# Moving elementwise steps between VectorE and GpSimd in a scheduled four-layer attention kernel

## The chip, the core and the metric

The kernel runs on one core of one Trainium2 chip. The metric is the device time of one execution in microseconds (us). The core's engines run their own instruction streams and wait for each other by semaphores: TensorE (PE) for matmuls, ScalarE (ACT) for activations, VectorE (DVE) and GpSimd (POOL) for elementwise work, and SyncE (SP), which here only issues DMAs.

## The reference

x is one sequence of 2048 tokens with 512 features, in bfloat16. Two kinds of layer alternate, each added to its input after a layer normalization, and each kind is applied twice with the same weights. Heads: 32 of 16 features.

```python
x = x + A(layernorm(x)); x = x + B(layernorm(x))     # twice

def A(x):     # four segments of 512 tokens, M and z carried from one to the next
    for s in range(4):
        p = softmax(q_s @ k_s.T * scale + causal_mask);  a_dot = p @ v_s
        a_mem = (phi(q_s) @ M) / (phi(q_s) @ z + 1e-6)   # phi(t) = t + 1 if t > 0 else exp(t)
        o = g * a_mem + (1 - g) * a_dot                  # g = sigmoid(beta), by head
        M = M + phi(k_s).T @ v_s;  z = z + phi(k_s).sum()
    return o @ wo

def B(x):     # linear attention, not causal
    phi = lambda t: concat(softmax(t @ w_phi), softmax(-t @ w_phi))
    kv = phi(k).T @ v;  z = phi(k).sum()
    return ((phi(q) @ kv) / (phi(q) @ z + 1e-6)) @ wo
```

## The kernel before

The sequence is held in SBUF as X, 16 tiles of 128 tokens. The program first records every operation as a node of a graph: the tiles that it reads and writes, the engines on which it may run, and for each engine a duration and a function that issues it. `Graph.place` then takes a packed table (`ORDER`) that holds, for all operations, their order, the engine of each, and the buffer of each tile; `Graph.emit` writes out one stream per engine with the semaphore waits that follow. So the order of everything, the choice between engines and the buffers come from that table, and an operation can only stand on an engine for which it has an entry.

The steps that the change and the prediction speak of:

- `ln` normalizes one tile of 128 tokens: statistics on VectorE (L599, L600), then on GpSimd an addition of epsilon (L607) and the power -1/2 (L609), then `xn = (x - mean) * rstd` on VectorE (L620, tile p). A transpose follows, by DMA from SP (L364) or, for some tiles, on TensorE (L380) with an evacuation (L359 on ScalarE, L360 on VectorE, tile pX).
- `a_proj` projects K, Q and V of a segment (L341). `kmask` then multiplies K with four masks of heads (L686 on VectorE, or L688 on ScalarE for a few) into pQ, the weights of the score matmuls. `phi` computes phi(t) as min(max(t, 0) + 1, exp(t)): the exponential on ScalarE, the clamp (max and add, L674) and the minimum (L675) on VectorE.
- `a_att`: scores (L326), their exponentials on ScalarE (L351, tiles p and pP), the product with V (L326), the division (L393, L906) and, from the second segment on, the addition of the memory part (L910). `out_proj` multiplies with wo and adds to X (L961).
- `b_keys` and `b_query` do layer B: exponentials on ScalarE (L351), sums and divisions on VectorE (L1015, L1030, L1117), V into pT (L359 or L360), and the sum of the two halves of the numerator (L1123).

`D` is the PSUM buffer, of which there are four. GpSimd otherwise makes constants and clears buffers, most of it at the start. The functions that the change touches, and what calls them:

Of the kernel before, what the change touches and what calls it, by code (L numbers as in the profile page):

```python
# [10 lines left out]
ALU = mybir.AluOpType  # L11
# [5 lines left out]
D = 512  # L17
H = 32
# [279 lines left out]
class Kernel:  # L298
# [58 lines left out]

    def evac(self, out_ap, in_ap, n, reads, writes, opens=(), label="", fast=False):
        ch = {"act": (n / 1.2 + 51, lambda e: e.activation(out_ap(), in_ap(), ACT.Copy)),  # L359
              "dve": ((340 if fast else n / 0.96 + 65), lambda e: e.tensor_copy(out_ap(), in_ap()))}  # L360
        return self.g.op(ch, reads, writes, opens, label=label, port=fast)
# [232 lines left out]
    def ln(self, t, xT, flex=False, pe=False, root="pool"):  # L594
# [24 lines left out]
        else:  # L619
          v(lambda e: e.tensor_scalar(xn.t[:], self.X[:, t, :], self.mv[:, t, 0:1], self.rstd[:, t:t + 1],  # L620
                                    op0=ALU.subtract, op1=ALU.mult), 300,
# [45 lines left out]
    def phi(self, dst, src, e_, keys, c0, n):  # L667
# [6 lines left out]
        v(lambda e: e.tensor_scalar(cut(dst), cut(src), 0.0, 1.0, op0=ALU.max, op1=ALU.add), 68 + n / 3.84, S, D, label="phmax", port=True)  # L674
        v(lambda e: e.tensor_tensor(cut(dst), cut(dst), cut(e_), ALU.min), 68 + n / 1.92, D + E, D, label="phadd", port=True)  # L675

    def kmask(self, KM, KT, halves, act):
# [3 lines left out]
        for sl in range(4):  # L681
# [4 lines left out]
            ch = {"dve": (129 + n / 3.84, lambda e, sl=sl, out=out: e.tensor_scalar(out(), src(), self.m4[:, sl:sl + 1], None, op0=ALU.mult))}  # L686
            if act:
                ch["act"] = (93 + n / 1.2, lambda e, sl=sl, out=out: e.activation(out(), src(), ACT.Copy, scale=self.m4[:, sl:sl + 1]))  # L688
# [150 lines left out]
    def a_att(self, L, s, i0):  # L839
# [10 lines left out]
        for gg in range(2):  # L850
# [58 lines left out]
            if s >= 1:  # L909
                v(lambda e, part=part: e.tensor_tensor(part(o), part(o), part(tmp), ALU.add), 335, [o[gg], tmp], [o[gg]], label="oadd", port=True)  # L910
# [139 lines left out]
    def b_query(self, L, c, store):  # L1050
# [49 lines left out]
        for tt in range(4):  # L1100
# [21 lines left out]
            if not pair:  # L1122
              v(lambda e, Tm=Tm, o=o: e.tensor_tensor(o.t[:].rearrange("p (a c) -> p a c", a=4), half(Tm, 0), half(Tm, 1), ALU.add), 335, [Tm], [o], label="nadd", port=True)  # L1123
# [56 lines left out]

def basep(ap):
# [13 lines left out]
TOK = {0: ((0, 1, 2, 3),), 1: ((0, 1, 2, 3),), 2: ((0, 1, 2, 3),), 3: ((0, 1, 2), (3,))}  # L1195
PE_T = ({("xA", 0, t) for t in range(4)} | {("xB", L, 15) for L in range(2)} | {("a", L, 3, 2, 1) for L in range(2)}
# [10 lines left out]
c-q~01C%YvvUWtIvs$OSk8RtwZQHhO+qP}nwr$&fRlCpJnYnk?y!+O_-oMs;xqDYuRz^lfeDOu>tkrRVL1IV_0QI0g5Hx^>&<LVIV`u_Rp&2xXWDp(VLOiGjnV~wAhxkweBxHk<Py<Rq  # L1207
R%ih&p%o~o3AvyGRD^<12y#MeXal987PN&jPzl;W3@8f;pfD7H_Rs-pLs38|1~H*Bl!M~X5n@3d=mec1AtZwAkOQhfUFZ!dAr)BY0=Xdxe1{+K6RN^%2!uD_Krr-yx6l_1e1z067}CHX
0PG3_;3**Xhj-8qy1@__3Q6G^aOe&LAvfm1_wWfm!xtC@d9erdgo%(3d%-l!iNhcl22lp^1H$z%12@2Q3`c`dz)YMA&*23O#t9GvmOemn%m}&IJa`GOU?Y^kuP_|Oz$WO2{V|wAXex|`
qF4+^!Z%m~4n=}3Fb#&_e8|E!!*&<}L(z}6LP?wsJ760`qX9SvRzWHBCx**lCuD)yFbQYEK->iyRs+XbFc||eEzE!^7=%k9I*o<Xum;NGR1|1&5|qUPxEzXLK`e|FFdXK`wJ;3JVLm8>  # L1210
XQ4E%gF?6hD&k5Qj`MH?#-K_V4#vTJ91j675+}oc9EDThFzkl|cmy1bKnLI;B*f7eKt~}MBhnr?2{CCe&cWTV4`*Q_j75>i4`<^7*b9j<KkS1EI0iGpSk$O+F)YO;I2RjW6I_gouo^bR
g_sVSVpLd()$u$mz{6-TB}OKRXJ8fXqKP;T7r}Tez?R{1Jc3nlH>JWxSQ%?z3P_Dru`$NRwOA9Qz(qJf>o5vkfJ+buS5bXT$7*41tcwew9yZ5=6c^LOYKo76R0mt&IoOOXu^G0)E!Y}Q
;wjvSo6sMUV0es&$MFQV!M1n^{4oTh(sc->qZoh@@CNLm^SA@EvIH0rFW@oUircXr?xo|f4WnZkTtk=P3be<A7!5-)Hm#-b)B$(nYCMN~Fa{ojLwFX~;Ck$cJ@5>6!VTD(R$wGNjXg0L
uArTmo@HQdXcxxBmb8*mP-pCd4e26Y!pIm4yJCGxj@>XNMa5Rsi1twpN<}HK0bRzV7>D*#FYJwduqL&o+EkZnQ9FuDQLqjbWc6qX#iQJ;J6?q=cnvyJV!A;$X(@G~tGJ0aQv$k%*YPek
rzX^xhEgXQM$M=%wx=6-6K`P%+<|-8fjUwP8crjqDRrf5^cd4(H@c74X(Yv`6EKRN-~-HxPcb9Dz=!w@vtcGIK$-C+X2;&thk8;kDoCeb5GAB#G=Y{=dc2K~Fas8%@$?+W&^Q`MqbVJB
r~cHJ22ej*M`I}om7pWEo`%q1I!YVp4i=`8l!x7djg*Z|q)C*Wm7-&GoDNYA)`Jey7D`H~X&X(Zt@Ie4KoR<ciRc}D#*8d4drx0*I~8Kz@fGI4T=W+2P(GHM^3V@FOH=48zM<E+gU--h
+DRv<Fnde)=p@~z+famEp=30bp3!M4%F@s&x=P>h9G$02G>x9qbh=Ep=n%`qa<bc$kKW@0I?O&%F?vK<@Dlq>KauDuy}`@uF{Put^om~72TV^#*hf6d($YivK}G2+eW3jGg)&eFmYIE|
($tY9r@`zA{iGpmAmfyuU1NjT3lcPsGSWM|&fM}vFX;xGPYdWKW7L&(W8dfkNy-b~Nzp~hN(WeR%0$4BX<A6xs4O#dkPT%g*f3U(on&RHCmYE|u@P(r^<v#wZ$@l58^g-89;_l8&B{|5
%1*b~ZN}IDR)J2jiqwboW96tX%L6&75@n%dtUo)=j<cCGi)Pb4wx1PaIcO}q!ZK5FHjZ6ol6PWfSP7>1ImX#Nc8AR&!S1tCtTL5klD%R6>>+!=?y^Pnmd$04*hMyvy<&4IfZc>D^q9S7
^Vw5Yl`gOa>^xh@7O`rix#5Z}rdo{iv+N10PMQgB*hDsoJ!8*VZ5GIa*i;t6CbMbmAyi;>SSXvqR<Q8QvZd@1L}JU>bQXbiW=q&CHk*}Ui`h&TjzxsX%wfyf3^s>#VJlf>R+o)ud)O+r  # L1220
m#t>?nB`TN!yB+qEPzL04Ovwd$S1Hh>;r4WKC>3=Bm2TyvTrPue`TdvHP(uKXZ4vMkIs;X=l(pHy<m;mJNBLhaW}NQ5(~%uSVXp#wPv&UIyQp?59YIZQ#O;oWb0X39)U;XA-o)K&Z@H?
Y#Uq0f3osC5|7L`u=PA9tI4*rjVubU&MWXKyaun$>+l_HCyT{mux4x%+svl&(mW2U$z!uNEG{d?%kaBUi^pS4SaDv7Z(;R$72c3n<Ox|--iWtjyI6cykJsf<St3@MH{kc68lS@(^Qb%m
v}e)yCO(%p;U)NPwwagYt9Ue4im&F;c?_PIZQ)z_R<?jI<kR?co|MPu^LP!GfUn`ncw4rE&*!`NTAqqe;*<GOo}8!VJ9z@ulsDrEc?!OWU*p&LV!n)b=81S>-i0sWyLl3pf-UDO_)4CP
# [76 lines left out]
```

## Time and profile before

| what | value |
|---|---|
| runs | 456.9, 456.93 and 458.73 us; median 456.93 |
| span of the profiled execution | 454.8 us; no time of its own is listed beside it |
| clock granted to TensorE | 1.000 over the span |
| GpSimd: busy, instructions | 58.4 us, 146 |
| VectorE: busy, instructions | 403.1 us, 766 |

A page of the profile gives busy time, share of the span and number of instructions by engine. A row of a group has the source line, engine, operation, what is written from what, the shapes and the count; then the busy time of the group in us and the mean of one in ns; then the idle time of the engine just before these instructions and what ended it. A row of a timeline begins with start and length in us. A row of waits says who waited, for whom, the total in us, how often, and the longest. The end of a matmul is modelled, and a GpSimd span is rough.

### The profile page before, as it was taken

The page shows a single profiled execution, that of the slowest core. Times are in us where ns is not written, and L with a number is a line of the kernel's source. Part 1 is how long each engine was busy: PE and PEld are TensorE (multiplying, and loading weights), DVE is VectorE, ACT ScalarE, POOL GpSimd, SP SyncE. Part 2 cuts the span into 40 slices and gives each one's busy share as a digit, 9 for nine tenths or more (in the row PEclk, how much of TensorE's full clock was granted, in tenths as well). Part 3 has the DMA queues.
Part 4 walks back from the last instruction along what each step waited for, and adds up shares of the span by engine and source line. Part 5 has one row for each costly group of instructions (what it writes and reads, how often), then busy time and mean ns, then how long its engine had stood idle before and what let it go on. Part 6 is the DMA issues. An engine that isn't in the chain of part 4 may idle for free.

```text
span 454.8 us, 26184 instructions
## 1 busy us (share of the span) xinstructions
PE 427.2 (94%) x12085; PEld 289.5 (64%) x12085; DVE 403.1 (89%) x766; ACT 420.9 (93%) x584; POOL 58.4 (13%) x146
## 2 busy tenths in 40 slices
PE   8999999999999989989999998999999988999787
PEld 4756667767766666655556666677677666765444
DVE  7999999998798978869999997999898896788897
ACT  5999999999999997899999999999899999699992
POOL 3411014010101101100330112020020020110000
PEclk9999999999999999999999999999999999999999
DMA  8976655564247212101255668436232414300355
GB/s 251 217 165 100 99 93 109 107 87 80 45 76 111 38 40 50 13 3 27 62 111 86 85 97 103 71 87 81 57 50 49 109 19 63 46 17 4 49 91 180
DMA packets 105167, 36.71 MB, mean 81 GB/s; under 512 B 91730, under 2 KB 105058, under 8 KB 105058
## 3 DMA queue, kind: packets, MB, share of 16 engines
q1 hardware_dynamic: 104226, 34.50, 42.9%
q8 instruction: 95, 1.56, 1.4%
q10 hardware_dynamic: 800, 0.52, 0.4%
q14 instruction: 14, 0.11, 0.1%
q0 software_dynamic: 32, 0.02, 0.0%
HBM read 10.76 MB, written 6.55 MB: 38 GB/s over the span
## 4 chain that ended last, share of the span: by engine, by line
PE 61%; ACT 20%; DVE 12%; issue 3%; DMA 3%; POOL 1%; DVEq 0%
PE D L341 38%; PE D L326 22%; ACT p L351 11%; ACT pP L351 7%; DVE X L961 2%; DVE pQ L686 1%; DVE p L1117 1%; DVE stats L599 1%; DMA pX<-p 1%; DMA p<-p 1%; ACT pS L351 1%; DVE p L620 1%; DMA X<-in_A_x_dram 1%; DVE pK L360 1%; DVE p L906 1%
## 5 line engine op out<-in xcount | busy, mean ns | idle before, releaser
L351 ACT ACTIVATE p<-D 128x1024 bf16<-128x1024 f32 (+1 forms) x256 | 225.6, 934 | 10.8 <-PE D L341 4.9
L351 ACT ACTIVATE pP<-D 128x640 bf16<-128x640 f32 (+2 forms) x192 | 149.5, 828 | 7.2 <-PE D L326 5.9
L326 PE MATMUL D<-pK,pQ 64*128 64x128 bf16 (+6 forms) x1792 | 112.0, 227 | 4.2 <-ACT p L351 1.0
L326 PEld LDWEIGHTS D<-pK,pQ 64*128 64x128 bf16 x1792 | 67.0, 93 | 40.2 <-ACT pP L351 8.5
L326 PE MATMUL D<-pW,pP 64*128 64x50 bf16 (+1 forms) x3072 | 84.0, 181 | 3.4 <-issue 2.7
L326 PEld LDWEIGHTS D<-pW,pP 64*128 64x128 bf16 x3072 | 68.6, 93 | 9.2 <-issue 3.8
L607 POOL TENSOR_SCALAR rstd<-mv 128x1 f32<-128x1 f32 x60 | 17.0, 288 | 340.8 <-DVE mv L600 340.4
L326 PE MATMUL D<-pW,p 64*128 64x50 bf16 (+1 forms) x2048 | 50.4, 181 | 0.4 <-DVE pQ L686 0.2
L326 PEld LDWEIGHTS D<-pW,p 64*128 64x128 bf16 x2048 | 44.3, 93 | 3.9 <-issue 1.1
L599 DVE BATCH_NORM_STATS2 stats<-X 128x6 f32<-128x512 bf16 x63 | 42.3, 679 | 1.9 <-DMA X<-in_A_x_dram 1.6
L961 DVE TENSOR_TENSOR X<-X,D 128x1024 bf16<-128x1024 bf16 (+1 forms) x36 | 39.2, 1096 | 5.1 <-PE D L341 4.6
L326 PE MATMUL D<-tri,rep 64*128 64x64 bf16 (+1 forms) x384 | 40.1, 197 | 0.0
L341 PE MATMUL D<-pX,WA_k 64*128 64x512 bf16 (+1 forms) x288 | 37.4, 353 | 1.0 <-issue 0.5
L341 PE MATMUL D<-pX,WA_q 64*128 64x512 bf16 (+1 forms) x288 | 37.7, 353 | 0.6 <-issue 0.6
L609 POOL TENSOR_TENSOR rstd<-rstd,mhalf 128x1 f32<-128x1 f32 x60 | 35.9, 604 | 3.4
L341 PE MATMUL D<-WB_k,pX 64*128 64x512 bf16 (+1 forms) x288 | 33.8, 352 | 1.1 <-DMA pX<-p 0.4
L341 PE MATMUL D<-WA_o,p 64*128 64x512 bf16 (+1 forms) x288 | 33.2, 352 | 1.6 <-issue 0.8
L1015 DVE TENSOR_REDUCE pS<-p 128x64 f32<-128x1024 bf16 x28 | 33.4, 1211 | 0.9 <-ACT p L351 0.9
L341 PE MATMUL D<-WB_v,pX 64*128 64x512 bf16 (+1 forms) x288 | 33.3, 352 | 0.0
L341 PE MATMUL D<-WA_v,pX 64*128 64x512 bf16 x256 | 33.2, 377 | 0.0
L341 PE MATMUL D<-WB_o,p 64*128 64x512 bf16 (+1 forms) x288 | 32.5, 353 | 0.4 <-ACT p L351 0.3
L341 PE MATMUL D<-pX,WB_q 64*128 64x512 bf16 x256 | 32.5, 376 | 0.3 <-ACT p L351 0.3
(123 smaller groups left out, 665.5 us busy)
## 6 DMA issues: line engine op xcount, KB each, us to landing
v_rows<-pV SPq DMA_DIRECT2D x16, 272.0 KB, 3.6
pW<-v_rows SPq DMA_DIRECT2D x64, 68.0 KB, 2.7
out_dram<-X SPq DMA_DIRECT2D x7, 256.0 KB, 2.6
X<-in_A_x_dram SPq DMA_DIRECT2D x3, 512.0 KB, 7.7
pX<-in_B_wqkv_dram SPq DMA_DIRECT2D x3, 512.0 KB, 4.5
p<-p SPq DMA_TRANSPOSE x73, 3.2
pX<-p SPq DMA_TRANSPOSE x54, 3.6
WA_k<-in_A_wk_dram SPq DMA_DIRECT2D x2, 256.0 KB, 7.2
```

The source lines that it names most:

```text
L326: ins = e.matmul(out_ap, lhsT, rhs, start=st, stop=sp, tile_position=(basep(lhsT), basep(out_ap)))
L341: ins = e.matmul(out_ap, lhsT[64 * hf:64 * hf + 64], rhs[64 * hf:64 * hf + 64], start=k == 0 and i == 0, stop=k == 1 and i == len(lists[hf ...
L351: return self.g.op({"act": (dur, lambda e: e.activation(out_ap(), in_ap(), func, scale=scale))}, reads, writes, opens, label=label)
L360: "dve": ((340 if fast else n / 0.96 + 65), lambda e: e.tensor_copy(out_ap(), in_ap()))}
L599: v(lambda e: e.bn_stats(self.stats[:, t, :], self.X[:, t, :]), 602, [R("X", t)], [R("st", t)], label="bn")
L607: v(lambda e: e.tensor_scalar(rs, self.mv[:, t, 1:2], LN_EPS, None, op0=ALU.add), 170, [R("mv", t)], [R("rstd", t)], eng="pool", label="rstd")
L609: v(lambda e: e.tensor_tensor(rs, rs, self.mhalf[:], ALU.pow), 540, [R("rstd", t), R("mhalf")], [R("rstd", t)], eng="pool", label="rstd")
L620: v(lambda e: e.tensor_scalar(xn.t[:], self.X[:, t, :], self.mv[:, t, 0:1], self.rstd[:, t:t + 1], op0=ALU.subtract, op1=ALU.mult), 300, [ ...
L686: ch = {"dve": (129 + n / 3.84, lambda e, sl=sl, out=out: e.tensor_scalar(out(), src(), self.m4[:, sl:sl + 1], None, op0=ALU.mult))}
L906: v(lambda e, pvv=pvv, rden=rden, part=part: e.tensor_tensor(part(o).rearrange("p (a h d) -> p a h d", a=2, h=16), pvv()[:, :, :, 0:16], r ...
L961: self.v(lambda e: e.tensor_tensor(X(), X(), src(), ALU.add), 65 + 512 * n / 0.96, pr + xr, xr, label="res")
L1015: v(lambda e, E=E, k=k, Z=Z: e.tensor_reduce(Z.t[:, 64 * k:64 * k + 64], E.t[:].rearrange("p (a f h) -> p a h f", a=16, h=4), AX.X, ALU.ad ...
```

## The change

Four kinds of operation get a second entry, for GpSimd: the normalization `xn`, the key masks, the clamp in `phi`, and the two sums of halves (`oadd` in `a_att`, `nadd` in `b_query`). The table is replaced by another, which gives order, engines and buffers of all operations; nothing that is computed changes.

```diff
+    def vp(self, fn, dur, pdur, reads, writes, opens=(), label="", port=False):
+        return self.g.op({"dve": (dur, fn), "pool": (pdur, fn)}, reads, writes, opens, label=label, port=port)
...
-          v(lambda e: e.tensor_scalar(xn.t[:], self.X[:, t, :], self.mv[:, t, 0:1], self.rstd[:, t:t + 1],
-                                    op0=ALU.subtract, op1=ALU.mult), 300,
+          self.vp(lambda e: e.tensor_scalar(xn.t[:], self.X[:, t, :], self.mv[:, t, 0:1], self.rstd[:, t:t + 1],
+                                    op0=ALU.subtract, op1=ALU.mult), 300, p_one(512),
...
-        v(lambda e: e.tensor_scalar(cut(dst), cut(src), 0.0, 1.0, op0=ALU.max, op1=ALU.add), 68 + n / 3.84, S, D, label="phmax", port=True)
+        self.vp(lambda e: e.tensor_scalar(cut(dst), cut(src), 0.0, 1.0, op0=ALU.max, op1=ALU.add), 68 + n / 3.84, p_one(n), S, D, label="phmax", port=True)
...
+            ch["pool"] = (p_one(n), ch["dve"][1])
...
-                v(lambda e, part=part: e.tensor_tensor(part(o), part(o), part(tmp), ALU.add), 335, [o[gg], tmp], [o[gg]], label="oadd", port=True)
+                self.vp(lambda e, part=part: e.tensor_tensor(part(o), part(o), part(tmp), ALU.add), 335, P_ADD, [o[gg], tmp], [o[gg]], label="oadd", port=True)
...
-              v(lambda e, Tm=Tm, o=o: e.tensor_tensor(o.t[:].rearrange("p (a c) -> p a c", a=4), half(Tm, 0), half(Tm, 1), ALU.add), 335, [Tm], [o], label="nadd", port=True)
+              self.vp(lambda e, Tm=Tm, o=o: e.tensor_tensor(o.t[:].rearrange("p (a c) -> p a c", a=4), half(Tm, 0), half(Tm, 1), ALU.add), 335, P_ADD, [Tm], [o], label="nadd", port=True)
...
+def p_one(n):
+    return 165 + n / 1.15
...
+P_ADD = 1290.0
...
 ORDER = """
-c-q~01C%YvvUWtIvs$OSk8RtwZQHhO+qP}nwr$&fRlCpJnYnk?y!+O_-oMs;xqDYuRz^lfeDOu>tkrRVL1IV_0QI0g5Hx^>&<LVIV`u_Rp&2xXWDp(VLOiGjnV~wAhxkweBxHk<Py<Rq
...
+c-qx@1DGaR(r!c?pDb6kZQHhO+dXY_+O}=mwrx(^wr5&5^Q)fOo|*k;clPdmp8w`km6=C@HzMA1vWh`;$PdXO1!RR75ECRMf+Ua_;zBHl2iYMP03?OnkPLD{d`JL!paK+viclB`N<t~94mF@ARDxPi
...
```

The added lines shift the source lines after them by 4 or 5 (by 8 at the file's end): the normalization is L624 after the change, the masks L690, the clamp L678, the sums L915 and L1128, epsilon and power L611 and L613, the evacuations L363 and L364; L326, L341 and L351 keep their numbers.

What moved, at three places. The first is the start of TensorE's stream, where `onesb` rows are warming matmuls, `ident` rows the first four transposes (eight matmuls each) and WA_k the first projection. Before:

```order
L701 MATMUL D<-onesb 128x256 x8
L380 MATMUL D<-ident,p 128x64 x8
L701 MATMUL D<-onesb 128x512 x4
L380 MATMUL D<-ident,p 128x64 x8
L701 MATMUL D<-onesb 128x512 x2
L380 MATMUL D<-ident,p 128x64 x8
L701 MATMUL D<-onesb 128x512 x4
L380 MATMUL D<-ident,p 128x64 x8
L341 MATMUL D<-pX,WA_k 128x256
```

After the change:

```order
L706 MATMUL D<-onesb 128x256 x8
L706 MATMUL D<-onesb 128x512 x20
L384 MATMUL D<-ident,p 128x64 x8
L326 MATMUL D<-beta_sb,onesb 128x32
L384 MATMUL D<-ident,p 128x64 x16
L706 MATMUL D<-onesb 128x512 x4
L384 MATMUL D<-ident,p 128x64 x8
L341 MATMUL D<-pX,WA_k 128x256
```

The matmul with beta, which stood in the first projection, now stands behind the first transpose.

The second place is GpSimd's stream at the turn from the first layer B to the second layer A, with the normalizations of the second pass's first four tiles of tokens. Before, it holds only epsilon and power:

```order
L607 TENSOR_SCALAR rstd<-mv 128x1 x2
L609 TENSOR_TENSOR rstd<-rstd,mhalf 128x1 x2
L607 TENSOR_SCALAR rstd<-mv 128x1
L609 TENSOR_TENSOR rstd<-rstd,mhalf 128x1
L607 TENSOR_SCALAR rstd<-mv 128x1
```

After the change:

```order
L611 TENSOR_SCALAR rstd<-mv 128x1
L613 TENSOR_TENSOR rstd<-rstd,mhalf 128x1
L611 TENSOR_SCALAR rstd<-mv 128x1
L624 TENSOR_SCALAR p<-X,mv,rstd 128x512
L613 TENSOR_TENSOR rstd<-rstd,mhalf 128x1
L624 TENSOR_SCALAR p<-X,mv,rstd 128x512
L611 TENSOR_SCALAR rstd<-mv 128x1
L613 TENSOR_TENSOR rstd<-rstd,mhalf 128x1
L611 TENSOR_SCALAR rstd<-mv 128x1
L624 TENSOR_SCALAR p<-X,mv,rstd 128x512
L613 TENSOR_TENSOR rstd<-rstd,mhalf 128x1
L690 TENSOR_SCALAR pQ<-p,m 128x32x32
```

Three of the four normalizations of these tokens stand between the powers, and a mask behind them; VectorE keeps the fourth.

The third place is ScalarE's stream near the end of the second layer A, where the last attention scores and the keys of layer B are done. Before:

```order
L351 ACTIVATE p<-D 128x8x64 x4
L359 ACTIVATE pT<-D 128x16x64
L359 ACTIVATE pX<-D 128x2x4x64
L359 ACTIVATE pT<-D 128x16x64
L351 ACTIVATE pS<-pS 128x128 x2
```

After the change:

```order
L351 ACTIVATE p<-D 128x8x64 x3
L351 ACTIVATE pS<-pS 128x128
L363 ACTIVATE pT<-D 128x16x64
L351 ACTIVATE p<-D 128x8x64
L351 ACTIVATE p<-D 128x1024
```

One of the two evacuations into pT and the one into pX have left ScalarE here; VectorE's stream has them at this place (L364).

More of the change, by code (lines that the diff above doesn't have):

```diff
@@ L1211 @@
[L1211 to L1222, printed above, removed]
```

94 lines of the change are left out of this document (52 added, 42 removed).

## The prediction

> **What bounds the kernel now.** I read the page first: busy shares, then the chain that ended last.
>
> ```profile
> span 454.8 us, 26184 instructions
> PE 427.2 (94%) x12085; PEld 289.5 (64%) x12085; DVE 403.1 (89%) x766; ACT 420.9 (93%) x584; POOL 58.4 (13%) x146
> PE 61%; ACT 20%; DVE 12%; issue 3%; DMA 3%; POOL 1%; DVEq 0%
> ```
>
> Three engines are nearly full and GpSimd (POOL) is nearly empty. An average does not say which of the three sets the time, so the next view is busy time by stages of 20 us; its columns are the length, then PE, weight loads, VectorE (DVE), ScalarE (ACT) and GpSimd.
>
> ```profile
> 40.00:60.00 20.00, 18.87 (x626) 12.95 (x622) 19.30 (x41) 19.87 (x25) 0.00 (x0) 1.00 0.58 100
> 80.00:100.00 20.00, 19.96 (x650) 14.08 (x646) 19.24 (x32) 19.79 (x27) 0.00 (x0) 1.00 0.63 108
> 180.00:200.00 20.00, 19.84 (x350) 12.15 (x346) 16.73 (x35) 17.37 (x24) 1.57 (x4) 1.00 0.13 15
> 380.00:400.00 20.00, 18.77 (x507) 14.43 (x499) 13.67 (x23) 16.15 (x25) 1.64 (x4) 1.00 0.33 43
> 440.00:460.00 20.00, 10.74 (x198) 5.78 (x192) 11.45 (x16) 6.64 (x11) 0.00 (x0) 0.94 0.40 114
> ```
>
> In the attention stages (40 to 60, 80 to 100) ScalarE works 19.8 of 20 us and VectorE 19.2 or 19.3. Where only projections are left (180 to 200, 380 to 400) both have room, and the last stage drains. TensorE looks equally full at 80 to 100, but its ends are modelled: in the next fence eight 512-wide matmuls are given 1.04 us while the following matmuls start 0.87 us after them. So I take ScalarE as the bound of the attention stages. The list of waits agrees: TensorE waits for ScalarE's softmax results, and less for VectorE.
>
> ```profile
> 83.04 1.04 PE L341 MATMUL D<-WB_k,pX 64*128 64x512 bf16 x8
> 83.91 0.26 PE L326 MATMUL D<-pW,p 64*128 64x50 bf16 x8
> ...
> PEld D L326 <- ACT pP L351: 10.4, 34, 1.1
> PEld D L326 <- ACT p L351: 9.7, 29, 0.8
> PEld D L380 <- DVE p L620: 3.4, 7, 1.0
> PEld D L929 <- DVE p L1117: 2.4, 4, 0.9
> ```
>
> **What leaves VectorE.** The order counts what stands where. Normalizations on VectorE go from 63 to 15; 1024-wide key masks from 56 to 22, 512-wide ones from 14 to 8; clamps from 26 to 15; sums of halves lose 10.
>
> ```profile
> L620 DVE TENSOR_SCALAR p<-X,mv,rstd 128x512 bf16<-128x512 bf16 x63 | 25.9, 417 | 2.5 <-POOL rstd L609 2.5
> L686 DVE TENSOR_SCALAR pQ<-p,m 128x1024 bf16<-128x1024 bf16 x56 | 25.9, 475 | 0.0
> L674 DVE TENSOR_SCALAR p<-pK 128x1024 bf16<-128x1024 bf16 x12 | 5.0, 418 | 0.0
> L910 DVE TENSOR_TENSOR p<-p 128x512 bf16<-128x512 bf16 x24 | 9.9, 411 | 0.2
> ```
>
> I price each by busy time over count: 48 x 25.9/63 = 19.7 us; 34 x 25.9/56 = 15.7; the six narrow masks, at most as long as a wide one and in width half of it, 6 x 0.38 = 2.3; 11 clamps x 5.0/12 = 4.6; 10 sums x 9.9/24 = 4.1. Together 46.4 us.
>
> **What ScalarE gives to VectorE.** ScalarE goes from 586 to 578 instructions. Gone are two evacuations into pT, one into pV, one 1024-wide into p, three into pX; one 512-wide evacuation and one narrow mask also leave it, and one 512-wide evacuation comes to it. VectorE has the counterparts.
>
> ```profile
> L359 ACT ACTIVATE pT<-D 128x1024 bf16<-128x1024 f32 x7 | 7.2, 1022 | 0.0
> L359 ACT ACTIVATE pV<-D 128x1024 bf16<-128x1024 f32 x3 | 3.2, 1064 | 0.0
> L359 ACT ACTIVATE pX<-D 128x512 bf16<-128x512 bf16 x10 | 5.7, 596 | 1.3 <-PE D L380 1.3
> L360 DVE CAST pT<-D 128x1024 bf16<-128x1024 f32 x7 | 8.5, 1220 | 0.3 <-PE D L341 0.3
> ```
>
> ScalarE saves 2 x 1.03 + 1.07 + 1.03 (a 1024-wide one like pT's) + 3 x 0.57, and 0.6 for the remaining narrow ones: 6.5 us. VectorE pays 4 x 1.21, and some 0.4 for the net of the narrow ones: 5.2 us. Its balance so far is 46.4 - 5.2 = 41 us less.
>
> **What GpSimd pays.** It has never run these shapes here. The nearest rows are its selects and one-element operations.
>
> ```profile
> L525 POOL TENSOR_SCALAR_AFFINE_SELECT p<-p 128x128 bf16<-128x128 bf16 x1 | 0.3, 292 | 0.1
> L509 POOL TENSOR_SCALAR_AFFINE_SELECT H<-ones 128x8 f32<-128x8 f32 x1 | 0.2, 185 | 0.0
> L607 POOL TENSOR_SCALAR rstd<-mv 128x1 f32<-128x1 f32 x60 | 17.0, 288 | 340.8 <-DVE mv L600 340.4
> L609 POOL TENSOR_TENSOR rstd<-rstd,mhalf 128x1 f32<-128x1 f32 x60 | 35.9, 604 | 3.4
> ```
>
> From 8 to 128 elements the select grows by 107 ns, 0.89 ns an element, so one input of 512 is 0.185 + 504 x 0.00089 = 0.63 us and of 1024 is 1.09 us. For a sum with two inputs the low end is that 0.63, the high end twice it, 1.27; I take the high end, since the two-input row is twice the one-input row even at one element. That is 56 x 0.63 + 44 x 1.09 + 10 x 1.27 = 96 us beside the 58 that it has: a third of the span, on an engine of its own. I cost it at nothing where VectorE and ScalarE cover it. Without that cover each moved instruction costs what it is longer, 0.2 us for a normalization and 0.6 us for a wide mask, and the transposes that SP issues next, or the score matmuls, wait.
>
> **The port.** The trace shows what happens when both engines work in SBUF.
>
> ```profile
> 21.71 1.00 POOL L553 MEMSET pW<- 128x1088 f32 x1
> 21.89 0.97 DVE L686 TENSOR_SCALAR pQ<-p,m 128x512 bf16<-128x512 bf16 x1
> 35.99 1.26 DVE L620 TENSOR_SCALAR p<-X,mv,rstd 128x512 bf16<-128x512 bf16 x1
> 36.10 1.00 POOL L553 MEMSET pW<- 128x1088 f32 x1
> 100.88 0.66 DVE L1030 TENSOR_TENSOR p<-p,pS 128x1024 bf16<-128x1024 bf16 x1
> 101.05 0.57 POOL L607 TENSOR_SCALAR rstd<-mv 128x1 f32<-128x1 f32 x1 [24.79 <-DVE mv L600]
> ```
>
> A mask of some 0.38 us and a normalization of 0.42 took 0.97 and 1.26, until just after the memset ended: held by 0.59 and 0.84, say 0.7 us each. The other way round, GpSimd's one-element operation ended 0.08 us after VectorE's two-input product. The order leaves VectorE some 190 instructions that read SBUF by itself twice or in that fast form. GpSimd's 96 us are 0.21 of the span, so 40 of them would meet a GpSimd instruction, and a chance start waits half of its mean 0.9 us: 18 us; with a few that wait longer I take 20. The ends are 0 (none meet) and 75 (each of the 110 new GpSimd instructions holds one VectorE instruction for 0.7). At 20, VectorE's balance is 21 us less work and waiting: still relief.
>
> The Trainium skill, "SBUF — State Buffer", section "Who interferes with whom", says that GpSimd and a VectorE instruction in a two-port mode or with two SBUF inputs share one port pair as an exclusive lock, and that the later one blocks for the whole instruction. The trace agrees for masks and normalizations (0.97 and 1.26 us); for two-input VectorE instructions held by GpSimd no row here shows it. With the rule for all of them VectorE loses the 20 us of the sum; by the memset rows alone, which show only the fast form (60 of the 190), it loses some 6, and the forecast would be about 1 us lower.
>
> **Two places on the path.** At the start the beta matmul now stands ahead of three of the four first transposes on TensorE, and its load behind a weight load on SP. At the turn from the first layer to the second three of the four normalizations stand in GpSimd's queue between the roots.
>
> ```profile
> WA_k<-in_A_wk_dram SPq DMA_DIRECT2D x2, 256.0 KB, 7.2
> 8.17 0.29 PE D L380 x8
> ...
> 213.15 1.23 DVE X L961
> ...
> 220.89 0.43 DVE p L620
> ```
>
> If beta lands only with the weights, 7.2 us after an issue at some 2.3, that is 9.5 against the 8.17 at which a transpose runs now: between 0 and 1.3 us late. I take 0.4, nearer to 0, as it is 32 values. At the turn the chain from the residual sum to the last normalization is 8.15 us now. With three normalizations of 0.63 between four pairs of add and root GpSimd's own work there is 4 x 0.89 + 3 x 0.63 = 5.5 instead of 3.6; most of it lies beside VectorE's next residual sum, and VectorE has three normalizations of 0.42 less there: between -1.3 and 1.9, and I take 0.2, near the middle.
>
> **Sum.** ScalarE's 6.5 us count in full, as it is the full engine where they lie. Of the 5.8 us that TensorE's transposes wait for VectorE's p I take 0.5, as the port gives back half of the relief. 454.8 - 6.5 - 0.5 + 0.4 + 0.2 = 448.4 us of span. The median of the runs, 456.93, is 2.1 above this execution's span; with the same 2.1 the time is 450.5.
>
> **Rivals.**
> *More than ScalarE's share.* If collisions are few, all 5.8 us of those two wait rows go too: 456.93 - 6.5 - 5.8 = 444.6. For it: GpSimd is idle 87%. Against it: 110 instructions that hold the port.
> *No change.* TensorE is the bound: 61% of the chain and 19.96 of 20 us at 80 to 100. Then ScalarE's 6.5 us become waiting for matmuls, and the time is 456.5 or so. Against it: 0.87 us of spacing under 1.04 of busy.
> *Slower.* The port holds VectorE more than it is relieved. The point is 41 / 0.7 = 59 holds. If 75 of the 110 hold it, VectorE has 11 us more than now; it is near full in about half of the stages, so 6 us come on the path, ScalarE's gain is lost behind late evacuations, and the time is 463. For it: in both quoted meetings the VectorE instruction waited nearly the whole memset. Against it: chance meetings give 40. This is the case that the skill's rule on the port pair speaks for.
>
> **How the numbers follow.** My forecast has a chance of 0.46, with 447 to 454.5 as its own range; more gain 0.17; no change 0.17; slower 0.20. Half a percent, 2.3 us, is about what a measurement of this kernel can tell from no change. Faster is 0.46 + 0.17 = 0.63, within it 0.17, slower 0.20. The range leaves out the lower half of the second case and the upper half of the slower one: 444 to 462.
>
> **What would show it.** ScalarE busy near 414 us and VectorE near 362 plus the holds; GpSimd near 154, with normalizations at 0.63 and wide masks at 1.09. The mean of VectorE's remaining masks, clamps and two-input products above 0.48, 0.42 and 0.69 would size the holds: 0.1 us more on 190 is the 20 us. TensorE's waits for p of L620 should turn into waits for GpSimd. The forecast fails if GpSimd's wide masks take 2 us, if its queue delays normalizations by several us, or if ScalarE's idle time grows by what its work shrinks.

## The result, and the profile after

The changed kernel takes 512.88 us (median of 4 runs, 510.9 to 519.61); the kernel before took 457.31 beside it on the same chip. The ratio is 1.12, with a 95% interval of 1.1149 to 1.1252; the run of 519.61 us was in a slower state and is not in the ratio. The change makes the kernel 12% slower: 55.6 us. I had forecast 450.5, with a range of 444 to 462.

From the page of the profile after: the span, the busy times, the slices of TensorE, GpSimd and the granted clock, and the chain that ended last.

```profile
span 511.2 us, 26165 instructions
PE 447.0 (87%) x12085; PEld 285.8 (56%) x12085; DVE 393.0 (77%) x667; ACT 418.2 (82%) x576; POOL 323.0 (63%) x253
...
PE   8968787699899899998797999989798888899897
...
POOL 3999999917787552201759978876998809260020
PEclk9989989889999999999898999999799999999999
...
PE 40%; POOL 26%; DVE 15%; ACT 10%; issue 4%; DMA 4%; SPq 1%; DVEq 0%; POOLq 0%
```

GpSimd went from 58 us of work to 323, not to the 154 of the forecast, and from 1% of the chain to 26%. In the slices it is full from the second to the eighth and again in several later stretches, and TensorE's digits are low there. The groups of instructions, for GpSimd and then for what stayed on VectorE (behind the bar: busy us, mean ns, idle before):

```profile
L624 POOL TENSOR_SCALAR p<-X,mv,rstd 128x512 bf16<-128x512 bf16 x48 | 104.0, 2168 | 2.3
L690 POOL TENSOR_SCALAR pQ<-p,m 128x1024 bf16<-128x1024 bf16 x34 | 100.6, 2965 | 10.7 <-DVE p L364 5.5 <-ACT p L363 5.2
...
L624 DVE TENSOR_SCALAR p<-X,mv,rstd 128x512 bf16<-128x512 bf16 x15 | 8.9, 598 | 9.1 <-POOL rstd L613 9.1
L690 DVE TENSOR_SCALAR pQ<-p,m 128x1024 bf16<-128x1024 bf16 x22 | 13.3, 609 | 0.1
L679 DVE TENSOR_TENSOR p<-p 128x1024 bf16<-128x1024 bf16 x22 | 18.1, 825 | 5.4 <-POOL p L678 5.0 <-ACT p L351 0.3
```

A normalization takes GpSimd 2.17 us, where I had 0.63. The wide masks take 2.97 (100.6 us for 34), where I had 1.09, and the clamps 3.71 and 3.68. Only the sums, 1.18 and 1.37, came out as priced. The same normalization on VectorE, 0.42 us before, is now 0.60: some of the few that stayed are held. The list of waits shows where this arrives; its first row here is from the kernel before, the others are from the changed one:

```profile
ACT pP L351 <- PE D L326: 5.9, 15, 0.9
...
ACT pP L351 <- PE D L326: 41.1, 45, 5.3
PEld D L326 <- POOL pQ L690: 12.2, 6, 3.4
PE D L341 <- DMA pX<-p: 10.8, 8, 3.5
DVE p L624 <- POOL rstd L613: 9.1, 5, 4.8
```

ScalarE, which I took for the bound, waits 41.1 us for score matmuls instead of 5.9, and the weight loads of these wait 12.2 us for masks on GpSimd. By stages of 20 us, with the columns as before; the first two rows are from the kernel before, the three behind the dots from the changed one:

```profile
20.00:40.00 20.00, 18.79 (x532) 13.38 (x530) 19.19 (x44) 19.05 (x25) 5.85 (x10) 1.00 0.80 143
360.00:380.00 20.00, 18.37 (x665) 13.87 (x661) 17.47 (x31) 19.49 (x26) 3.37 (x9) 1.00 0.33 65
...
20.00:40.00 20.00, 15.95 (x340) 10.23 (x336) 13.87 (x33) 14.55 (x19) 19.65 (x18) 0.91 0.62 92
80.00:100.00 20.00, 13.46 (x400) 8.94 (x392) 11.86 (x20) 13.31 (x19) 19.60 (x14) 0.97 0.23 52
360.00:380.00 20.00, 16.65 (x454) 10.99 (x452) 13.75 (x21) 13.76 (x19) 19.75 (x11) 0.83 0.29 32
```

In these three stages of the changed kernel GpSimd works 19.6 to 19.8 of 20 us, and every other engine has room. At 80 to 100 TensorE fell from 19.96 to 13.46 and ScalarE from 19.79 to 13.31. The granted clock, 1.00 in all these stages before, is 0.83 to 0.97.

### The profile page after: what moved, and what is told of

Read it like the earlier page. It is cut to its first block, busy times and chain, and to the rows that moved or that the text cites. A ratio compares the mean times of both kernels' runs of the same rounds, so it can differ in the third digit from the quotient of the medians.

```text
span 511.2 us, 26165 instructions
## 1 busy us (share of the span) xinstructions
PE 447.0 (87%) x12085; PEld 285.8 (56%) x12085; DVE 393.0 (77%) x667; ACT 418.2 (82%) x576; POOL 323.0 (63%) x253
## 4 chain that ended last, share of the span: by engine, by line
PE 40%; POOL 26%; DVE 15%; ACT 10%; issue 4%; DMA 4%; SPq 1%; DVEq 0%; POOLq 0%
PE D L341 25%; PE D L326 12%; POOL pQ L690 9%; POOL p L624 9%; ACT p L351 7%; POOL p L678 4%; ACT pP L351 3%; POOL rstd L613 3%; DMA pX<-p 2%; PE D L706 2%; DVE p L1122 2%; DVE X L966 1%; DVE pQ L690 1%; DVE stats L603 1%; POOL rstd L611 1%
## 5 line engine op out<-in xcount | busy, mean ns | idle before, releaser
L351 ACT ACTIVATE p<-D 128x1024 bf16<-128x1024 f32 (+1 forms) x256 | 224.9, 929 | 24.4 <-PE D L326 12.5
L351 ACT ACTIVATE pP<-D 128x768 bf16<-128x768 f32 (+2 forms) x192 | 149.1, 817 | 42.3 <-PE D L326 41.1
L326 PE MATMUL D<-pK,pQ 64*128 64x128 bf16 (+6 forms) x1792 | 111.2, 231 | 29.3 <-POOL pQ L690 10.1
L690 POOL TENSOR_SCALAR pQ<-p,m 128x1024 bf16<-128x1024 bf16 (+1 forms) x41 | 112.3, 2746 | 10.7 <-DVE p L364 5.5
L624 POOL TENSOR_SCALAR p<-X,mv,rstd 128x512 bf16<-128x512 bf16 x48 | 104.0, 2168 | 2.3
L326 PEld LDWEIGHTS D<-pK,pQ 64*128 64x128 bf16 x1792 | 65.2, 95 | 62.9 <-POOL pQ L690 12.2
L326 PE MATMUL D<-pW,pP 64*128 64x50 bf16 (+1 forms) x3072 | 85.0, 182 | 2.1 <-issue 1.3
L326 PEld LDWEIGHTS D<-pW,pP 64*128 64x128 bf16 x3072 | 68.3, 93 | 9.0 <-issue 2.7
L611 POOL TENSOR_SCALAR rstd<-mv 128x1 f32<-128x1 f32 x60 | 16.1, 273 | 82.2 <-DVE mv L604 81.8
L326 PE MATMUL D<-pW,p 64*128 64x50 bf16 (+1 forms) x2048 | 50.5, 182 | 0.4 <-issue 0.2
L326 PEld LDWEIGHTS D<-pW,p 64*128 64x128 bf16 x2048 | 44.4, 94 | 4.8 <-ACT p L351 0.6
L341 PE MATMUL D<-pX,WA_q 64*128 64x512 bf16 (+1 forms) x288 | 40.4, 381 | 2.5 <-DMA pX<-p 2.2
L1128 POOL TENSOR_TENSOR p<-p 128x512 bf16<-128x512 bf16 x4 | 5.5, 1372 | 57.4 <-DVE p L1122 57.4
L341 PE MATMUL D<-pX,WA_k 64*128 64x512 bf16 (+1 forms) x288 | 37.5, 358 | 3.8 <-DMA pX<-p 3.5
L326 PE MATMUL D<-tri,rep 64*128 64x64 bf16 (+1 forms) x384 | 39.8, 202 | 0.0
L341 PE MATMUL D<-WB_k,pX 64*128 64x512 bf16 (+1 forms) x288 | 33.9, 358 | 5.5 <-DMA pX<-p 5.1
L341 PE MATMUL D<-WB_o,p 64*128 64x512 bf16 (+1 forms) x288 | 35.3, 368 | 2.3 <-DMA p<-p 0.7
L613 POOL TENSOR_TENSOR rstd<-rstd,mhalf 128x1 f32<-128x1 f32 x60 | 35.0, 591 | 2.8
L341 PE MATMUL D<-WA_o,p 64*128 64x512 bf16 (+1 forms) x288 | 33.5, 353 | 1.2 <-issue 0.7
```

The costliest lines, as they stand in the source:

```text
L326: ins = e.matmul(out_ap, lhsT, rhs, start=st, stop=sp, tile_position=(basep(lhsT), basep(out_ap)))
L341: ins = e.matmul(out_ap, lhsT[64 * hf:64 * hf + 64], rhs[64 * hf:64 * hf + 64], start=k == 0 and i == 0, stop=k == 1 and i == len(lists[hf ...
L351: return self.g.op({"act": (dur, lambda e: e.activation(out_ap(), in_ap(), func, scale=scale))}, reads, writes, opens, label=label)
L611: v(lambda e: e.tensor_scalar(rs, self.mv[:, t, 1:2], LN_EPS, None, op0=ALU.add), 170, [R("mv", t)], [R("rstd", t)], eng="pool", label="rstd")
L613: v(lambda e: e.tensor_tensor(rs, rs, self.mhalf[:], ALU.pow), 540, [R("rstd", t), R("mhalf")], [R("rstd", t)], eng="pool", label="rstd")
L624: self.vp(lambda e: e.tensor_scalar(xn.t[:], self.X[:, t, :], self.mv[:, t, 0:1], self.rstd[:, t:t + 1], op0=ALU.subtract, op1=ALU.mult), ...
```

## The experiments

Four theories stood at the start. Theory 1: GpSimd's own price of these instructions makes it the bound. Theory 2: GpSimd's instructions are long only because VectorE works beside them. Theory 3: the new order is bad, whoever does the work. Theory 4: what costs is VectorE held at the shared port. Every run was compared with the kernel before on the same chip (454.6 to 457.3 us). Where a kernel begins with fills of buffers (so that nothing undefined is read), its first load is issued later, and I take the difference off; that the rest moves by just as much is assumed. In the changed kernel and in the run with quarters:

```profile
0.79 0.46 SPq L466 DMA_DIRECT2D X<-in_A_x_dram  x1
```

```profile
5.46 0.46 SPq L470 DMA_DIRECT2D X<-in_A_x_dram  x1
```

That is 4.7 us; 0.8 where only the normalizations are cut.

| kernel | time, us | above the kernel before | less fills |
|---|---|---|---|
| changed kernel | 512.9 | 55.6 | |
| new table, all back on VectorE | 552.4 | 97.3 | |
| same, sums left on GpSimd | 544.0 | 88.9 | |
| same, normalizations left on GpSimd | 521.0 | 65.9 | |
| same, masks left on GpSimd | 550.3 | 95.2 | |
| new table sorted by start, all back | 477.3 | 21.8 | |
| the same, moved work cut to 1/16 | 476.6 | 21.1 | 16.4 |
| new table unsorted, all back, cut to 1/16 | 548.2 | 91.7 | 87.0 |
| changed kernel, GpSimd's work cut to 1/4 | 475.0 | 19.3 | 14.7 |
| changed kernel, cut to 1/16 | 473.9 | 19.3 | 14.6 |
| only normalizations cut to 1/4 | 487.3 | 32.7 | 31.9 |
| only masks cut to 1/4 | 496.1 | 41.5 | 36.8 |
| same time on GpSimd, hardly any data | 510.9 | 56.3 | 51.6 |
| masks as a product of two operands | 513.2 | 56.7 | |
| old order, all 110 moved | 537.3 | 81.7 | |
| old order, sums moved | 458.1 | 2.5 | |
| old order, 17 moves with slack | 457.2 | 0.7 | |
| old order, nothing moved, cut to 1/16 | 459.2 | 2.7 | -2.0 |

### Giving the operations back

The first four kernels change only the engine, in `place`; order and buffers are those of the changed kernel. The tuple names the kinds given back:

```diff
             o.seq, o.eng = k, ENGS[raw[2 * n + o.id]]
+            if o.eng == "pool" and "dve" in o.ch and o.label in ("xn", "Km", "phmax", "oadd", "nadd"):
+                o.eng = "dve"
```

> The order and the buffers of the changed kernel, with all 110 moved operations (48 normalizations, 41 key masks, 11 clamps, 10 sums) given back to VectorE. Theory 1 (GpSimd's own price of these instructions, 2.1 to 3.7 us each where 0.6 to 1.1 were reckoned, makes it the bound of some stages): the loss goes, 447 to 465 us, most likely 456. Theory 2 (GpSimd's instructions are long because VectorE works beside them): the same. Theory 3 (the new order itself is bad, whichever engine does the work): 500 to 515 us.

> As the run with all given back, but the 10 sums of halves stay on GpSimd (1.2 to 1.4 us each there, 0.4 on VectorE). Theory 1: within 2 us of the run with all given back, on either side, because a sum costs on GpSimd about what was reckoned. Theory 4 (what costs is that GpSimd holds VectorE at the shared port): at most 10 holds of 0.8 us more, so 0 to 8 us above it. Theory 3: 500 to 515 us.

> As the run with all given back, but the 48 normalizations stay on GpSimd: 48 x 2.17 = 104 us of work there. Theory 1: 10 to 30 us above the run with all given back, lost in the first 100 us and at the turn of the layers, where several normalizations stand in a row ahead of TensorE's transposes; away from there nothing. Theory 4: 48 holds of up to 0.8 us on VectorE, spread over the whole span, 5 to 15 us. Theory 3: as the run with all given back, 500 to 515 us.

> As the run with all given back, but the 41 key masks stay on GpSimd: 34 x 2.97 + 7 x 1.68 = 112 us of work there. Theory 1: 10 to 35 us above the run with all given back, in waits of TensorE for the masks (the new kernel has 12.2 us of them), and the granted clock lower in the stretches where TensorE waits. Theory 2: the masks' mean falls toward 1.1 us, since less else is on GpSimd to collide with VectorE. Theory 4: 0 to 10 us. Theory 3: as the run with all given back, 500 to 515 us.

Measured: 552.35, 544.01, 521.04 and 550.27 us. Theory 1, as I had it, missed by nearly 90 us: without any move the new order is slower than with all of them. Theory 3's range, 500 to 515 us, was missed too. Left on GpSimd, the sums came out 8 us and the normalizations 31 us below the first run, where Theory 1 had them within 2 us and 10 to 30 us above; the masks 2 us below and not 10 to 35 above. Theory 2 fell: alone on GpSimd the masks' mean was 3.02 us, not 1.1. These four cannot price the parts, as the sorted table shows below.

### The price, measured by itself

A ladder of instructions in place of the computation: the three forms, a flat mask, a product and sums on GpSimd alone, then on VectorE alone, then both at once.

> Not the computation: a ladder of instructions. First GpSimd alone with VectorE idle: the normalization's, mask's and clamp's form at 128 to 1024 columns, the mask's as one product with a broadcast operand, sums. Then VectorE alone, then both at once. Theory 1 (the price is GpSimd's own): alone it takes 2.0 to 2.2 us for the normalization of 512, 2.7 to 3.0 for the mask of 1024, 3.5 to 3.7 for the clamp of 1024, and within 15% of that beside VectorE. Theory 2 (VectorE's work stretches it): alone 0.6, 1.1 and 1.1 us. Theory 4 (port): beside GpSimd, VectorE's normalizations and sums with both operands in the main memory are stretched by about 0.8 us in some or all cases, its statistics and casts out of the accumulators by nothing.

GpSimd alone, VectorE idle: the normalization's form at three widths, from the groups in the window of that phase.

```profile
L29 POOL TENSOR_SCALAR g<-gx,mv 128x512 bf16<-128x512 bf16 x4 | 8.2, 2072 | 14.2 <-DVE vx L85 14.2
L29 POOL TENSOR_SCALAR g<-gx,mv 128x256 bf16<-128x256 bf16 x4 | 4.8, 1218 | 0.0
L29 POOL TENSOR_SCALAR g<-gx,mv 128x128 bf16<-128x128 bf16 x4 | 3.1, 792 | 0.0
```

And from the groups of the whole run three that ran only in that phase: L32 is a mask without the layout, L33 the clamp's form, L35 the mask as a product of two operands, the second of them the mask's column spread by a step of zero.

```profile
L32 POOL TENSOR_SCALAR g<-gx,mv 128x1024 bf16<-128x1024 bf16 x4 | 11.3, 2842 | 0.0
L33 POOL TENSOR_SCALAR g<-gx 128x512 bf16<-128x512 bf16 x4 | 7.6, 1918 | 0.0
L35 POOL TENSOR_TENSOR g<-gx,mv 128x1024 bf16<-128x1024 bf16 x4 | 7.4, 1892 | 0.0
```

The price is GpSimd's own. From 256 to 512 columns the normalization grows by 3.3 ns an element; the mask, with one operation where the normalization has two, takes 2.84 us for 1024. In the later phase, beside VectorE's own normalizations, the mean was 2.09 us; beside statistics and casts out of the accumulators 2.07 to 2.16; beside VectorE's 1024-wide products 2.57, beside two-input sums 2.72. These last two are 24 and 31% above GpSimd alone, more than the 15% that I had allowed; still, Theory 2 is out for most of the price.

### GpSimd's work made short, engines and order kept

GpSimd computes only the first columns, in the new order on the new engines. Readers of a normalization read a constant tile, readers of a clamp the exponential, so that nothing undefined is read; every wait stays.

```diff
-  xn.t[:],        self.X[:, t, :]
+  xn.t[:, 0:128], self.X[:, t, 0:128]     # 32 in the second run; masks and clamps alike
```

> The changed kernel with its order, engines and buffers as they are, but each normalization, mask and clamp on GpSimd covers only a quarter of its columns, so that it takes about the 0.6 and 1.1 us that the new code reckons with (p_one); what reads a normalization's or a clamp's tile reads a constant or the exponential instead, and a few us of fills stand ahead of the program. This leaves out part of the computation. Theory 1 (GpSimd's price of these instructions is what makes the changed kernel slow; its order is good at the price that it reckons with): 440 to 465 us. Theory 3 (the new order is bad by itself, as 552 us with all given back to VectorE suggests): 490 us or more.

> As the run with a quarter of the columns, but a sixteenth: every moved normalization, mask and clamp on GpSimd is now about as short as it was on VectorE, or shorter (0.3 to 0.6 us). This leaves out part of the computation. If what the quarter run still has above the kernel before (475 us, of which some 4.7 are its fills) is the rest of the price: 457 to 464 us. If it is the new order itself (Theory 3 in a smaller size): it stays at 468 to 475 us.

Measured: 474.95 (ratio 1.0436, interval 1.0362 to 1.051) and 473.89 us (1.0421, 1.0357 to 1.0485). With the quarter a normalization took 0.85, a wide mask 1.05 and a clamp 1.16 to 1.18 us, where the new code reckons with 0.61, 1.06 and 1.06. The time lies between the two ranges that I had put down, 440 to 465 and 490 or more. So some 41 of the 55.6 us are the price. Making the work shorter still brings nothing: some 15 us stay (12 to 19 by the first interval, less fills), and they are not GpSimd's length.

> The changed kernel with only the 48 normalizations on GpSimd cut to a quarter of their columns (2.17 us to 0.85); masks and clamps whole; readers read a constant. This leaves out part of the computation. Theory 1: GpSimd has 63 us less, of which a part is on the chain: 485 to 503 us. Theory 3: 505 us or more.

> The changed kernel with only the 41 key masks on GpSimd cut to a quarter of their columns (2.97 and 1.68 us to 1.05 and 0.63); normalizations and clamps whole; a few us of fills stand ahead. This leaves out part of the computation. Theory 1: GpSimd has 72 us less: 485 to 503 us. With the run on the normalizations the two should make up most of the 43 us between the changed kernel and the quarter run. Theory 3: 505 us or more.

Measured: 487.26 and 496.1 us. Short normalizations alone bring 55.6 - 31.9 = 23.7, short masks alone 55.6 - 36.8 = 18.8. Their sum, 42.5, is about the 41 of both with the clamps; each has 3 to 4 us of noise, so what the clamps cost can't be told from nothing.

### The port

GpSimd busy as long, but with powers of one element, which move hardly any data:

```diff
+  ins = e.tensor_tensor(d[:, k:k + 1], self.one1[:], self.mhalf[:], ALU.pow)   # 4, 5 or 3, and 6 times
```

> The changed kernel with each moved normalization, mask and clamp on GpSimd replaced by 4, 5 (3 for the narrow ones) and 6 powers of 128x1 of about 0.59 us, so that GpSimd is busy about as long but moves hardly any data; what reads a normalization's or a clamp's tile reads a constant or the exponential, and a few us of fills stand ahead. This leaves out part of the computation. Theory 1 (GpSimd's time alone): 505 to 525 us. Theory 4 (GpSimd holds VectorE at the port; the moved kernel's VectorE instructions are stretched by about 15 us): lower by that, 490 to 505 us, and VectorE's normalization and sums back at 0.41 us.

Measured: 510.87 us, 51.6 above the kernel before with the fills off. The page's row of busy times:

```profile
PE 445.2 (88%) x12085; PEld 284.9 (56%) x12085; DVE 384.8 (76%) x669; ACT 418.3 (82%) x576; POOL 316.1 (62%) x605
```

VectorE is busy 384.8 us, 3.5 of them fills, against 393.0: the port stretched it by some 12 us in the changed kernel. Its normalizations are back at 0.46 us, its minimum at 0.68. About 4 us of time go with this (and with GpSimd's own 7 us less), no more than the two intervals (1.1078 to 1.1288 here, 1.1149 to 1.1252 there) can tell from none. With hardly any data moved nearly all of the loss is still there; Theory 4 is not what made the kernel slow.

The mask as a product is a third shorter in the ladder and computes the same:

```diff
-  e.tensor_scalar(out(), src(), self.m4[:, sl:sl + 1], None, op0=ALU.mult)
+  e.tensor_tensor(out(), src(), self.m4[:, sl:sl + 1].to_broadcast(...), ALU.mult)
```

> The changed kernel with GpSimd's 41 key masks written as one product of two operands (the mask's column spread by a step of zero) in place of a product with a column as scalar; the same result. Alone, the flat form took 1.89 us at 1024 columns as a product and 2.84 as the scalar form. Theory 1: a mask takes 1.9 to 2.2 us, GpSimd has 28 to 40 us less, and since cutting the masks by 72 us brought 21, 8 to 12 us of it reach the end: 500 to 506 us. If the price were not what holds: 510 to 515 us.

Measured: 513.24 us, no gain (ratio 1.127, 1.1199 to 1.1341): in the range that I had put down for the case that the price is not what holds. GpSimd's masks did get shorter; VectorE's normalizations and sums beside them got longer:

```profile
L691 POOL TENSOR_TENSOR pQ<-p,m 128x1024 bf16<-128x1024 bf16 x34 | 66.9, 1980 | 14.0 <-DVE p L364 8.3 <-ACT p L363 5.7
...
L624 DVE TENSOR_SCALAR p<-X,mv,rstd 128x512 bf16<-128x512 bf16 x15 | 13.9, 933 | 9.0 <-POOL rstd L613 9.0
L915 DVE TENSOR_TENSOR p<-p 128x512 bf16<-128x512 bf16 x18 | 12.4, 693 | 0.3
```

GpSimd's busy time fell from 323.0 to 286.1 us and VectorE's rose from 393.0 to 416.7. I take it that one ate the other, which is argued and not shown; which form holds the port how long was not measured apart.

### The old order

The same moves with the order and buffers of the kernel before: all 110, then the 10 sums, then 17 operations (9 normalizations, 7 masks, 1 clamp) picked for a late reader.

```diff
+            if o.id in MOVED:
+                o.eng = "pool"
```

> The order and the buffers of the kernel before, with the same 110 operations on GpSimd. Theory 1: the price acts here too: GpSimd is given 110 operations of 2 to 3.7 us, 265 us in all, at places that were chosen for VectorE's 0.4 to 0.5 us, so 490 to 540 us, with waits for GpSimd on the chain. Theory 3: what costs is the new order, so the old one with the same moves stays at 455 to 470 us.

> The order and the buffers of the kernel before, with only the 10 sums of halves on GpSimd (1.2 to 1.4 us there, 0.4 on VectorE), so VectorE loses 4.1 us. Theory 1: no price that was missed, little slack to be won: 453 to 460 us, likeliest 456. Theory 4 (holds at the shared port): up to 8 us above the kernel before.

> The order and the buffers of the kernel before, with only 17 operations on GpSimd (9 normalizations, 7 masks, 1 clamp): those whose result is not read for a long time in the old order, one at a time, away from GpSimd's powers. VectorE is rid of some 8 us. Theory 1: nothing waits for them, so within 1% of the kernel before, 453 to 459 us, and no gain, since VectorE is not the bound. Theory 4: 17 holds of up to 0.8 us, 0 to 10 us above it.

Measured: 537.31, 458.14 (ratio 1.0063, 1.0033 to 1.0093) and 457.21 us (1.0012, 0.9978 to 1.0047). The price acts in the old order too; there the weight loads of the score matmuls wait 26.7 us for masks on GpSimd, against 12.2. The new order softens the moves by 26 us (81.7 against 55.6 above the kernel before). The ten sums cost 0.3 to 0.9%, small and clear of the noise. Where only what has slack is moved, no loss and no gain can be told from the noise.

What VectorE's relief is worth was measured with nothing on GpSimd: in the old order the 100 moved normalizations, masks and clamps stay on VectorE, cut to a sixteenth.

> The order and the buffers of the kernel before, nothing on GpSimd, but the 100 normalizations, masks and clamps that the change moves are cut on VectorE to a sixteenth of their columns, so that VectorE is rid of some 30 us at no price; readers of a normalization or clamp read a constant or the exponential, and some 4.7 us of fills stand ahead. This leaves out part of the computation. It measures what the relief of VectorE is worth by itself. If it is worth what the forecast took (6 us, through work given on from ScalarE, which is not given on here): 452 to 458 us with the fills. If VectorE's relief is worth nothing, ScalarE and TensorE being the bound: 458 to 462 us. If VectorE was a bound after all: 445 us or less.

Measured: 459.23 us, less fills 454.6 against 456.5. By the ratio's interval (1.0051 to 1.012) less the fills it lies between 2.3 us faster and 0.8 slower. That is for some 17 us of VectorE's busy time (403.1 against 389.3, 3.5 of that fills).

```profile
PE 426.4 (93%) x12085; PEld 286.6 (63%) x12085; DVE 389.3 (85%) x768; ACT 421.0 (92%) x584; POOL 62.4 (14%) x148
```

### Why the first run took 552 us

The same cut on VectorE in the new order, all given back:

> The order and the buffers of the changed kernel with all 110 operations given back to VectorE, the 100 normalizations, masks and clamps among them cut to a sixteenth of their columns; a few us of fills stand ahead. This leaves out part of the computation. If the 14 us that the changed kernel keeps with nearly free GpSimd work are the new order's own: 470 to 482 us. If they come of what is left on GpSimd: 455 to 464 us.

Measured: 548.2 us, far above both ranges. VectorE's load is not what made the 552, then. What is left is the place. The table is one list; of an operation on GpSimd only the place among GpSimd's own counts, so it may stand behind others that start later. On VectorE, which works in order, it then comes late. For the last two kernels I sorted the list by the start of each operation as the table's own durations give it. With the changed kernel's engines every queue keeps its sequence; only then were the operations given back, whole and cut.

> The changed kernel's order and buffers with all 110 operations given back to VectorE, whole, as in the first run of this study, but the table is first sorted by when each operation would start by the table's own durations; with the changed kernel's engines this leaves each engine's queue exactly as it was. If the 552 us came of late places in VectorE's queue: 457 to 480 us, likeliest 468. If the new queues of the other engines are bad by themselves, or VectorE can't carry its work in them: 500 us or more.

> As the run before it, but the 100 normalizations, masks and clamps among them are cut on VectorE to a sixteenth of their columns, and a few us of fills stand ahead. This leaves out part of the computation. If the 14 us that stay with nearly free work on GpSimd (474 us with the fills) belong to the new queues of the other engines: 468 to 476 us. If they belong to what GpSimd still does: 457 to 463 us.

Measured: 477.31 (ratio 1.0479, 1.044 to 1.0519) and 476.62 us (1.0466, 1.0418 to 1.0514). The first is in the range for late places, the second just above the range for the new queues. The list's places made 75 us of the 552. The page of the first of the two:

```profile
span 479.4 us, 26137 instructions
PE 440.3 (92%) x12085; PEld 282.6 (59%) x12085; DVE 409.7 (85%) x777; ACT 417.6 (87%) x576; POOL 55.7 (12%) x143
```

Two things follow. On these queues VectorE does the moved work 34 us faster than GpSimd (21.8 us above the kernel before, against 55.6). And 16 us stay even with the work cut on VectorE and nothing long on GpSimd, like the 15 with it cut on GpSimd: they belong to the new table, to its queues or its buffers. So Theory 1 holds for 41 of 55.6 us and Theory 3 for about 15.

No run of its own settles what in the new table costs the 15, but the traces point to one place. TensorE is busy 438.3 us in the cut run against 427.2 before, though the durations of its matmuls add up to about the same (2715 and 2705 us): fewer of them overlap. In both kernels a projection is recorded as two halves, and the second waits by a semaphore for the first:

```python
        o1 = self.g.op({"pe": (dur, half(0))}, reads, writes, opens, label=label, rows=64)
        return self.g.op({"pe": (dur, half(1))}, reads, writes, label=label + "2", rows=64, hard=o1)
```

Of 158 such pairs, 5 stand side by side in TensorE's queue before; between the halves of the others stands other work. In the new table 63 stand side by side. The weight loads that wait for TensorE's own projection, in the kernel before and in the cut run:

```profile
PEld D L341 <- PE D L341: 2.2, 5, 0.6
...
PEld D L348 <- PE D L348: 26.1, 63, 1.0
```

All fourteen runs with the new table have 63 such waits (25.7 to 26.6 us), all five with the old one 5 or 6 (2.2 to 2.8). From the start of a half of eight 512-wide matmuls to the start of TensorE's next work it is 1.09 us where that waits so, and 0.86 where nothing waits; with 256 columns it is 0.67 and 0.44. My estimate from such differences is 13.7 us of TensorE's time in the cut run and 1.2 before: most of the 15, if all of it reaches the end. No run parts the halves, so this is read from the traces and not shown by a change.

## Why the prediction was wrong, step by step

**What GpSimd pays** is the step that failed first: the largest term, mis-sized, and with it the cover that I costed at nothing. I drew a line through the selects (292 ns at 128 elements, 185 at 8) to 0.63 and 1.09 us. A select of 128 columns is no row for a multiply of 1024: the same widths take 2.07 and 2.84 us with GpSimd alone. The 96 us became 323.0 - 58.4 = 265, and "costed at nothing where covered" fell with it: no cover was left from 20 to 100 us. The failure sign I had named, wide masks of 2 us, is what came (2.97). With GpSimd's work cut to a price near my reckoning the kernel took 470 with the fills taken off, so even that would not have saved the forecast: the new order is the second step that failed, below.

The Trainium skill, "GPSIMD Engine Reference", section 4.1, calls one-input elementwise work on GpSimd "roughly line-rate" against VectorE and two-input work about twice as slow. Here the measurement decides the other way round: the one-input normalization takes 2.07 us against VectorE's 0.41, five times; the two-input sum 1.18 to 1.37 against 0.41, three times.

**What leaves VectorE.** The count was right, the worth was not. I added up durations, 46.4 us, for a balance of 41 less. VectorE's instructions overlap one another (before, their durations add up to 449 us and its busy time is 403.1), so busy time falls by less: without the holds, in the run with powers, it is 381.3 with the fills taken off, 22 us below the kernel before. And relief is worth little here: 17 us of busy time brought 2.3 us at most in the old order.

**ScalarE's 6.5 us** "in full". ScalarE's busy time fell by 2.7, and none of it shows: with all work back on VectorE it is at 417.6 in a span of 479.4. No run lightens ScalarE alone, so whether its work would come off one to one as long as it is the full engine stays open; here it no longer was.

**The port.** I took 20 us of holds on VectorE; it was some 12 of busy time, with the signs that I named (masks from 0.48 to 0.61, the two-input minimum, L675 and now L679, from 0.68 to 0.83). The mechanism stood, but that the size is near is luck: by my own working GpSimd's real 265 us, 0.52 of the span, would have met 99 of the 190 instructions and held each for half of 2.4 us, some 119 us in all. It was not what decided, as about 4 us reach the end. The Trainium skill, "SBUF — State Buffer", section "Who interferes with whom", has the later engine block for the whole instruction. In the ladder this does not hold: of 70 normalizations of VectorE beside GpSimd's of 2.09 us (203 to 240 us) 34 took 0.40 us, 35 took 0.74 to 0.85 and one 1.17 (0.61 in the mean), so a hold cost 0.34 to 0.45 us, that one aside, and never GpSimd's whole time. Each held one ended 0.93 us after a normalization began on GpSimd, or 0.16 us after the next one began, and others ran free in between.

**The two places.** At the head the first projection starts at 11.52 instead of 9.24 us, 2.3 late and not 0.4; the beta matmul, which I feared, ran 0.11 us behind the first transpose and did not wait. The first transpose itself came at 9.95 instead of 7.39 us; until then TensorE worked through warming matmuls without a pause. At the layer turn the chain from the residual sum to the last normalization is 12.2 us (240.65 to 252.87) and not 8.2: three normalizations of 2.1 us stand in GpSimd's part of it (242.90 to 252.43). I had bounded it at 1.9 more.

**The rivals.** The slower one was right in sign and wrong in mechanism: it had the port, at 463, where GpSimd's own time did it. A rival in which the price is three times mine was missing; a range taken from rows of another operation should have carried it.

**The order.** I treated the new order as free. It costs some 15 us that no step of mine had; by my estimate from the traces most of it lies on projections whose two halves now stand side by side.

## What to carry to other kernels

Price an instruction on an engine from the same operation at the same width; where there is no such row, measure a ladder first, since GpSimd took five times VectorE's time where a neighbouring operation promised one and a half. Before paying anything for relief of a busy engine, cut its work for a look: here 17 us less on VectorE were worth 2.3 at most. A new order is a change of its own: even with GpSimd's work short it cost some 15 us here. Judge order and placement apart, look for waits of an engine for its own work, and sort the list before an operation changes its queue.

## What the runs showed of the hardware

GpSimd took longer for a product with a column as scalar (2.84 us for 1024) than for the same product of two operands, the second the column spread by a step of zero (1.89). And VectorE can shut GpSimd out. In the ladder, while VectorE ran 84 two-input sums of 512 in a row, undisturbed at 0.41 us each, one single mask stood on GpSimd for 35 us (the window 262 to 290 us). The sums ran from 259.5 to 293.1 us; the mask began at 260.8 and ended 2.7 us after the last of them, about as long as a mask takes alone (2.84):

```profile
L30 POOL TENSOR_SCALAR g<-gx,mv 128x1024 bf16<-128x1024 bf16 x1 | 35.0, 35005 | 0.0
L34 DVE TENSOR_TENSOR v<-vx 128x512 bf16<-128x512 bf16 x84 | 28.2, 412 | 0.0
```

Normalizations on GpSimd beside the same sums, earlier in that run, took 2.72 us, so it is not every instruction. The granted clock was 0.83 to 0.97 in seven stages of 20 us of the changed kernel, the last stage aside. In six of them TensorE was busy for 13.5 to 16.7 of the 20 us; the seventh (100 to 120, TensorE 19.35) follows right behind one. At 40 to 60 TensorE was busy for 16.4 and the clock stayed at 1.00, so a busy share alone does not tell it. In the run with all given back, at a mean clock of 0.935, TensorE was busy 461.9 us, against 427.2 before for the same instructions; how much of that is the clock and how much lost overlap was not measured apart.
